# Batch 1's retention steps moved ahead inside batch 0's second product, on a one-core retention-and-mixer kernel

## The chip, the cores and the metric

The kernel runs on one core of a Trainium2 chip. The metric is device time in microseconds (us), the median of several executions. One further execution was taken with the hardware profiler; all rows quoted below are from it. The engines are named as in the profile: PE is TensorE's matrix multiply and PEld its weight load, DVE is VectorE, ACT is ScalarE, POOL is GpSimd, SP is SyncE (here only a queue that issues DMA transfers).

## The reference

```python
# q, k, v: (4, 8, 768, 64): batch, heads, sequence, head size
gamma = 1.0 - 2.0 ** (-5.0 - np.arange(H))
for t in range(S):                                   # retention, a recurrent state per head
    state = gamma * state + k[:, :, t] (outer) v[:, :, t]
    y[:, :, t] = 1/sqrt(D) * q[:, :, t] @ state
x = y.transpose(0, 2, 1, 3).reshape(B, S, H * D)     # (4, 768, 512)
h = x.transpose(0, 2, 1) @ U @ V                     # low-rank mixing along the sequence, rank 32
u = x + h.transpose(0, 2, 1)
out = u + relu(u @ w_ch1) @ w_ch2                    # 512 -> 2048 -> 512
```

## The kernel before

The sequence of 768 is cut into six chunks of 128 rows. For a chunk `c` of batch `b`, retention does the following steps.

- `ret_in`: GpSimd scales the loaded keys and queries by powers of gamma (`ret_k`, L257, writes `kd`; `ret_q`, L262, writes `qd`). For batch 1 and chunks 2, 3 and 4 it also queues on SP the loads of batch 2's chunks 0, 1 and 2 (`load_chunk`).
- `ret_T` (L424): eight PE transposes put `qd` and `kd` into one PSUM bank; `evict` copies them to the tile `qkT`, on ACT or DVE, whichever a small cost model (`Balance.pick`) expects to be done first.
- `ret_S` (L437): eight matmuls give the scores in two banks; DVE masks them into `a` (L446).
- `ret_v` (L268): ACT casts the values to `vb`.
- `ret_O`: matmuls give the chunk's outputs from the running state and from `a` and `vb`, and add to the state's sum; ACT evicts the outputs to `x` (L463), DVE evicts the state (L482).

After all six chunks of a batch come its mixing steps (`mix_P`, `mix_n`, `mix_u`), and then the two products of the mixer. The first product (`mlp1`) has 32 slots. The second has 42: three sets of row blocks (`i` = 0, 1, 2), each with seven products of half-size blocks in the order 4, 5, 1, 2, 3, 7, 6, each product split into two slots of four matmuls of 256 columns. A set's additions are shared out: ACT copies products 4, 5, 1 and 2 from PSUM (L642), GpSimd adds 5, 1 and 2 in four adds and one late add (L646), and DVE adds 3, 7 and 6 straight from PSUM (L646). Ahead of the second product DVE forms sums of the weights (`w2_sum`, L578) and of the activations (`g_sums`, L593).

Everything is issued in program order on every engine, and the program order comes from a table: `weave` runs through the slots, and ahead of each slot emits the actions that `put` has hung on it. So batch 1's retention is laid between the slots of batch 0's second product. In the table `at` gives the slot of each chunk's transposes, `lead` how many slots ahead `ret_in` is emitted, `S_at` and `O_at` the slots of scores and outputs, and `mix_at` the start of mixing; `n1` is 32, the first slot of the second product. `ret_v` goes three slots ahead of `O_at`. An action that is emitted later on GpSimd's queue runs later there, whether or not its inputs have long been there. POOL and SP have one queue each.

In what follows "slot 11" means slot `n1 + 11`, and T0, S0 and O0 are the transposes, scores and outputs of batch 1's chunk 0.

Of the kernel before, what the change touches and what calls it, by code (L numbers as in the profile page):

```python
# [47 lines left out]
def kernel(  # L48
# [52 lines left out]
    def set_banks(main, mix=None):  # L101

        for who, banks in (("main", main), ("mix", mix)):
            use[who] = banks and sorted(banks, key=lambda i: taken.get(i, 0))
            n_use[who] = 0
# [33 lines left out]
    def load_chunk(b, c, kinds="kqv"):  # L139
        t = staged.setdefault((b, c), {})  # L140
        for nm in kinds:
            load_one(t, b, c, {"k": k, "q": q, "v": v}[nm], nm + "_n")
# [8 lines left out]
    def load_w1(lo, w):  # L151
        nc.gpsimd.dma_start(
            out=w1b[:, :, ds(lo, w)],
            in_=moe_w_ch1[:, ds(lo, w)].rearrange("(c p) m -> p c m", p=P))

    def load_w2(s):
        nc.gpsimd.dma_start(
            out=w2b[:, ds(4 * s, 4)],
            in_=moe_w_ch2[ts(s, 512)].rearrange("(j p) c -> p j c", p=P))
# [9 lines left out]
    for what in ("q0", "kA", "q1", "k2", "k3", "vA", "q2", "k4", "v2", "k5", "v3", "v4", "v5"):  # L169
        src, i = {"q": q, "k": k, "v": v}[what[0]], what[1]  # L170
# [351 lines left out]
    def by_token(b, j):  # L522
        return b >= 2 or (b == 1 and j >= NCK // 2)
# [6 lines left out]
    def mix_r(b, j):  # L530
        h = mm_bank("mix")
        matmul(h, Vb[:, ts(j, P)], Ps[b], DM, start=True, stop=True)
        nc.vector.tensor_tensor(res_of(b, j), h, xs[b, j], op=ALU.add)  # L533
        bal.book("V", 0.69)
# [17 lines left out]
    def mlp1_two(b, ms, hf):  # L552
        if b not in gTs:
            gTs[b] = gtp.tile([P, NM, S], bf16, tag="gT", name=f"gT_{b}")
        g = [mm_bank()[:, :HS] for _ in ms]
        for cs in ((0, 1), (2, 3)):
            for m, o in zip(ms, g):
                for c in cs:
                    matmul(o, w1b[:, c, ts(m, P)], uTs[b][:, c, ts(hf, HS)], HS, start=(c == 0),
                           stop=(c == NCB - 1))  # L560
        for m, o in zip(ms, g):
            evict(gTs[b][:, m, ts(hf, HS)], o, HS, relu=True)
# [9 lines left out]
    def w2_sum(i, h):  # L572
        b11, b12, b21, b22 = (x[:, ts(h, HM // 2)] for x in w2_quads())
        z = w2s[:, :, ts(h, HM // 2)]
        o, x, y, op = ((z[:, 2], b21, b22, ALU.add), (b21, b21, b11, ALU.subtract),
                       (z[:, 0], b11, b22, ALU.add), (z[:, 1], b11, b12, ALU.add),
                       (b12, b12, b22, ALU.subtract))[i]
        nc.vector.tensor_tensor(o, x, y, op=op)  # L578
        bal.book("V", 0.65)
# [3 lines left out]
    def g_sums(b, n, which=range(5), w=2):  # L583
        if b not in gss:
            gss[b] = sump.tile([P, 3, HM, HS], bf16, tag="gs", name=f"gs_{b}")
        g, s = gTs[b], gss[b]
        mu, ml = ds(w * n, w), ds(HM + w * n, w)
        a11, a12, a21, a22 = (g[:, m, ts(t, HS)] for t in (0, 1) for m in (mu, ml))
        sums = ((s[:, 2, mu], a11, a12, ALU.add), (s[:, 0, mu], a11, a22, ALU.add),
                (s[:, 1, mu], a21, a22, ALU.add), (a12, a12, a22, ALU.subtract),  # L590
                (a21, a11, a21, ALU.subtract))
        for o, x, y, op in (sums[i] for i in which):
            nc.vector.tensor_tensor(o, x, y, op=op)  # L593
            bal.book("V", 0.55)
# [4 lines left out]
    def free_from(banks):  # L599
        free_banks[:] = sorted(banks, key=lambda i: taken.get(i, 0))  # L600
# [82 lines left out]
    def mlp1_slots(b):  # L683
        if b == 0:
            ms = [m + x for m in range(0, HM, 2) for x in (0, 1, HM, HM + 1)]
            return [lambda m=m, hf=hf: mlp1(b, m, hf) for m in ms for hf in (0, 1)]
        early = [m + x * HM for m in range(HM // 2) for x in (0, 1)]
        late = [m + HM // 2 for m in early]
        return [lambda m=m, hf=hf: mlp1(b, m, hf)
                for m, hf in [(m, hf) for hf in (0, 1) for m in early]  # L690
                + [(m, hf) for m in late for hf in (0, 1)]]
# [19 lines left out]
    def put(side, i, f):  # L711
        side.setdefault(int(i), []).append(f)

    def ret_side(b, at, lead, S_at, O_at, side):


        for c in range(NCK):
            put(side, max(0, at[c] - lead), lambda c=c: ret_in(b, c))
            put(side, O_at[c] - 3, lambda c=c: ret_v(b, c))
        for cs in S_at:  # L720
            put(side, S_at[cs], lambda cs=cs: ret_S(b, cs))
        for f, when in ((ret_T, at), (ret_O, O_at)):
            for c in range(NCK):
                put(side, when[c], lambda c=c, f=f: f(b, c))
        if by_dma(b) and b + 1 < B:
            for c, i in enumerate((31, 36, 41)):
                put(side, i, lambda c=c: load_chunk(b + 1, c))
        return side
# [67 lines left out]
    for b in range(B):  # L796
        nxt = b + 1 < B
        slots = mlp1_slots(b)
        n1 = len(slots)
        side = {}  # L800
        set_banks([0, 1, 2, SA, SB, OB])
        if b == 0:
            taken.update({i: n for n, i in enumerate((1, 2, 0, OB, SA, SB, TP))})
            set_banks([1, 2, 0, OB, SA, SB, TP])
            slots[:4] = [lambda: mlp1_two(0, (0, 1), 0), lambda: None,
                         lambda: mlp1_two(0, (0, 1), 1), lambda: None]
            for i, s in ((1, 512), (2, DH // 2 + 512)):
                put(side, i, lambda s=s: load_w1(s, 512))
            for n, s in enumerate((0, 2, 1, 3)):
                put(side, 4 + n, lambda s=s: load_w2(s))  # L810
            for c, nm in ((0, "kq"), (1, "kq"), (2, "kq"), (0, "v"), (3, "kq"), (1, "v"), (4, "kq"),
                          (2, "v"), (3, "v"), (5, "kq"), (4, "v"), (5, "v")):
                put(side, 14, lambda c=c, nm=nm: load_chunk(1, c, nm))
            for j, i in enumerate((4, 6, 8, 13, 14, 15)):
                put(side, i, lambda j=j: mix_r(0, j))
            for n, i in enumerate((9, 17, 25)):
                put(side, i, lambda n=n: g_sums(0, n))
            for i in range(5):
                put(side, 22, lambda i=i: w2_sum(i, 0))
            for i in (0, 1):  # L820
                put(side, n1 - 2, lambda i=i: w2_sum(i, 1))
            for f, *args in ((g_sums, 0, 3, (0, 1)), (w2_sum, 2, 1), (g_sums, 0, 3, (2,)),
                             (w2_sum, 3, 1), (w2_sum, 4, 1), (g_sums, 0, 3, (3, 4))):
                put(side, n1, lambda f=f, args=args: f(*args))
            at, lead, mix_at = [n1 + i for i in (11, 14, 18, 22, 26, 30)], 4, n1 + 36
            S_at = {(c,): n1 + i for c, i in enumerate((14, 17, 21, 25, 29, 33))}
            O_at = [n1 + i for i in (18, 21, 25, 29, 33, 36)]
        if b == 1:
            slots[:2] = [lambda: mlp1_two(1, (0, HM), 0), lambda: None]
            for j in range(NCK):  # L830
                if not by_token(1, j):
                    put(side, 6 + 3 * j, lambda j=j: mix_r(1, j))
        if b:
            for n, i in enumerate((13, 17, 25, n1)):
                put(side, i, lambda n=n: g_sums(b, n))
        if b and nxt:
            set_banks([0, 1, 2, TP])
            put(side, 22, lambda: set_banks([0, 1, 2]))
            at, lead, mix_at = [10 + 4 * c for c in range(NCK)], 5, n1 + 21
            S_at = {(0, 1): 27, (2,): 36, (3,): 40, (4,): 44, (5,): 48}  # L840
            O_at = [31, 34, 41, 45, 49, 53]
        banks = [[0, 1, 2], [0, 1, 2, TP], [0, 1, 2, TP], [0, 1, 2, TP, SA, SB, OB, ST]][b]
        put(side, n1, lambda: free_from(banks))
        if nxt:
            ret_side(b + 1, at, lead, S_at, O_at, side)
            put(side, mix_at, lambda: use.update(mix=[SA, SB, OB] + [TP] * (b == 0)))
            mix_side(b + 1, mix_at, side)
        if b in (1, 2):
            for c, i in ((3, 0), (4, 7), (5, 15)):
                put(side, i, lambda c=c: load_chunk(b + 1, c))  # L850
        weave(slots + mlp2_slots(b), side)
# [30 lines left out]
```

## Time and profile before

| | |
|---|---|
| median of 3 executions | 231.03 us (230.79 to 231.48) |
| profiled execution, its own time | 230.28 us |
| its span, first to last instruction | 228.5 us |
| PE busy | 215.0 us, 94% |
| DVE / ACT / POOL busy | 143.2 / 128.4 / 102.6 us |
| granted TensorE clock, mean over the span | 0.986 |

The time of an execution holds the span and 1.8 us around it. In the rows of a timeline the columns are the start in us from the span's start, the length in us, engine, line, operation, output and inputs with their shapes, and the count of instructions merged in the row; a bracket gives the idle time of that engine in front of the row and what ended it. PE's lengths are modelled and overlap: how long a piece of PE work takes is read from its start to the start of the next row. A row of the waits gives who waited for whom, the total, the number of times and the longest. A row of the windows gives a stretch of time, its length, busy time and count for PE, PEld, DVE, ACT and POOL, the granted clock (1.00 is full), the DMA share and GB/s.

### The profile page before, as it was taken

The page shows a single profiled execution, that of the slowest core. Times are in us where ns is not written, and L with a number is a line of the kernel's source. Part 1 is how long each engine was busy: PE and PEld are TensorE (multiplying, and loading weights), DVE is VectorE, ACT ScalarE, POOL GpSimd, SP SyncE. Part 2 cuts the span into 40 slices and gives each one's busy share as a digit, 9 for nine tenths or more (in the row PEclk, how much of TensorE's full clock was granted, in tenths as well). Part 3 has the DMA queues.
Part 4 walks back from the last instruction along what each step waited for, and adds up shares of the span by engine and source line. Part 5 has one row for each costly group of instructions (what it writes and reads, how often), then busy time and mean ns, then how long its engine had stood idle before and what let it go on. Part 6 is the DMA issues. An engine that isn't in the chain of part 4 may idle for free.

```text
span 228.5 us, 5097 instructions
## 1 busy us (share of the span) xinstructions
PE 215.0 (94%) x1997; PEld 151.2 (66%) x1999; DVE 143.2 (63%) x287; ACT 128.4 (56%) x267; POOL 102.6 (45%) x125
## 2 busy tenths in 40 slices
PE   7999999995798998999999999999999999999990
PEld 2566655664586874565788685657887865668890
DVE  8497668988278653298895633578983623555113
ACT  3377657762164647676646547776544757772220
POOL 6756910008959395332152359633606230006550
PEclk9999999999799999999999999999999999999997
DMA  6998999999999924999959988979560550000222
GB/s 173 244 261 172 168 174 207 200 219 225 205 260 227 232 84 127 193 161 173 107 123 221 261 168 154 227 132 171 101 132 3 161 160 4 1 0 3 93 92 93
DMA packets 100776, 34.90 MB, mean 153 GB/s; under 512 B 87152, under 2 KB 97808, under 8 KB 100752
## 3 DMA queue, kind: packets, MB, share of 16 engines
q1 hardware_dynamic: 94640, 30.29, 63.9%
q0 software_dynamic: 6112, 4.29, 12.9%
q8 instruction: 15, 0.25, 0.5%
q14 instruction: 9, 0.07, 0.1%
HBM read 27.46 MB, written 6.29 MB: 148 GB/s over the span
## 4 chain that ended last, share of the span: by engine, by line
PE 63%; POOL 11%; issue 10%; DMA 4%; DVE 4%; ACT 3%; SPq 3%; POOLq 0%; DVEq 0%; ACTq 0%
PE bk L116 61%; POOL s L646 4%; POOL res L646 4%; DMA k_n<-in_k_dram 2%; POOL qd L262 2%; DMA q_n<-in_q_dram 2%; SPq L288 2%; POOL kd L257 1%; SPq L136 1%; PE bk L424 1%; DVE a L352 1%; ACT st L299 1%; DVE res L646 1%; ACT x L538 1%; ACT kT L299 1%
## 5 line engine op out<-in xcount | busy, mean ns | idle before, releaser
L116 PE MATMUL bk<-uT,w1b 128*128 128x384 bf16 x512 | 86.4, 326 | 0.7 <-ACT uT L121 0.6
L121 ACT ACTIVATE gT<-bk 128x384 bf16<-128x384 f32 x123 | 60.1, 490 | 30.0 <-PE bk L116 29.9
L116 PEld LDWEIGHTS <-w1b 128*128 128x128 bf16 x512 | 49.8, 98 | 34.4 <-issue 1.6
L646 POOL TENSOR_TENSOR s<-s,s 128x256 f32<-128x256 f32 x24 | 18.2, 758 | 87.5 <-ACT s L642 65.1
L116 PEld LDWEIGHTS <-gT 128*128 128x128 bf16 x392 | 37.3, 99 | 8.4 <-issue 1.7
L593 DVE TENSOR_TENSOR gs<-gT 128x768 bf16<-128x768 bf16 x48 | 27.7, 614 | 20.8 <-ACT gT L121 20.3
L646 DVE TENSOR_TENSOR res<-bk,res 128x256 f32<-128x256 f32 x37 | 14.4, 420 | 28.1 <-PE bk L116 23.1
L116 PEld LDWEIGHTS <-gs 128*128 128x128 bf16 x288 | 27.3, 98 | 3.9
L257 POOL TENSOR_TENSOR kd<-k_n,Gk 128x512 bf16<-128x512 f32 x18 | 19.0, 1056 | 16.8 <-DMA k_n<-in_k_dram 11.1
L116 PE MATMUL bk<-w2b,gT 128*128 128x256 bf16 x192 | 26.4, 273 | 0.1
L116 PE MATMUL bk<-w2b,gs 128*128 128x256 bf16 x192 | 26.2, 273 | 0.0
L116 PE MATMUL bk<-w2s,gT 128*128 128x256 bf16 (+1 forms) x200 | 26.2, 277 | 0.0
L446 DVE TENSOR_TENSOR a<-bk,mask 128x512 bf16<-128x512 f32 x36 | 23.0, 684 | 4.8 <-PE bk L116 4.8
L642 ACT ACTIVATE s<-bk 128x256 f32<-128x256 f32 x36 | 13.5, 381 | 17.8 <-PE bk L116 17.3
L262 POOL TENSOR_TENSOR qd<-q_n,Gq 128x512 bf16<-128x512 f32 x18 | 19.8, 1098 | 5.7 <-DMA qkT<-qd 3.9
L533 DVE TENSOR_TENSOR res<-bk,x 128x512 f32<-128x512 f32 x24 | 15.8, 686 | 7.9 <-PE bk L116 7.6
L646 POOL TENSOR_TENSOR res<-res,s 128x256 f32<-128x256 f32 x24 | 17.9, 747 | 1.9
L593 DVE TENSOR_TENSOR gT<-gT 128x768 bf16<-128x768 bf16 x32 | 18.2, 609 | 0.0
L463 ACT ACTIVATE x<-bk 128x512 bf16<-128x512 f32 x18 | 10.7, 596 | 13.1 <-PE bk L116 10.4
L538 ACT ACTIVATE x<-res 128x512 bf16<-128x512 f32 x15 | 9.2, 628 | 6.3 <-DVE res L533 6.3
L116 PE MATMUL bk<-w2s,gs 128*128 128x256 bf16 x96 | 12.6, 273 | 0.0
L116 PEld LDWEIGHTS <-qkT 64*128 64x128 bf16 (+1 forms) x204 | 8.4, 95 | 4.7 <-issue 2.9
(98 smaller groups left out, 229.1 us busy)
## 6 DMA issues: line engine op xcount, KB each, us to landing
out_dram<-res SPq DMA_DIRECT2D x23, 256.0 KB, 2.3
k_n<-in_k_dram SPq DMA_DIRECT2D x22, 256.0 KB, 5.0
v_n<-in_v_dram SPq DMA_DIRECT2D x22, 256.0 KB, 4.7
q_n<-in_q_dram SPq DMA_DIRECT2D x18, 256.0 KB, 5.1
w2b<-in_moe_w_ch_dram POOLq DMA_DIRECT2D x4, 512.0 KB, 15.1
in<-in_q_dram SPq DMA_DIRECT2D x3, 512.0 KB, 6.4
w1b<-in_moe_w_ch_dram POOLq DMA_DIRECT2D x4, 256.0 KB, 5.5
w1b<-in_moe_w_ch_dram POOLq DMA_DIRECT2D x2, 512.0 KB, 9.0
```

The source lines that it names most:

```text
L116: nc.tensor.matmul(o, l, r, **kw)
L121: nc.scalar.activation(o, i, AF.Relu if relu else AF.Copy)
L257: eng.tensor_tensor(kd, k_n, Gk[:, c].unsqueeze(2).to_broadcast([P, H, D]), op=ALU.mult)
L262: eng.tensor_tensor(qd, rc[b, c]["q_n"], Gq[:, c].unsqueeze(2).to_broadcast([P, H, D]), op=ALU.mult)
L288: nc.sync.dma_start_transpose(out=qkT[:, i], in_=src.rearrange("p h d -> p (h d)"))
L446: nc.vector.tensor_tensor(r["a"][:, e], r["s"][e].rearrange("p (n t) -> p n t", n=NP), mask4, op=ALU.mult)
L463: nc.scalar.activation(x_of(b, c), o, AF.Copy)
L533: nc.vector.tensor_tensor(res_of(b, j), h, xs[b, j], op=ALU.add)
L538: nc.scalar.activation(xs[b, j], res[b, j], AF.Copy)
L593: nc.vector.tensor_tensor(o, x, y, op=op)
L642: nc.scalar.activation(t[nm], o, AF.Copy)
L646: eng.tensor_tensor(o, x, y, op=op)
```

## The change

Only the table for batch 1 inside batch 0's second product changes. The transposes move from slots 11, 14, 18, 22, 26, 30 to 8, 12, 16, 20, 25, 29; the lead grows from 4 to 5, so that `ret_in` moves from slots 7, 10, 14, 18, 22, 26 to 3, 7, 11, 15, 20, 24. The scores move from 14, 17, 21, 25, 29, 33 to 11, 15, 19, 23, 28, 32; the outputs from 18, 21, 25, 29, 33, 36 to 15, 19, 22, 27, 31, 35; mixing from 36 to 35. No instruction is added or taken away as computation.

```diff
-            at, lead, mix_at = [n1 + i for i in (11, 14, 18, 22, 26, 30)], 4, n1 + 36
-            S_at = {(c,): n1 + i for c, i in enumerate((14, 17, 21, 25, 29, 33))}
-            O_at = [n1 + i for i in (18, 21, 25, 29, 33, 36)]
+            at, lead, mix_at = [n1 + i for i in (8, 12, 16, 20, 25, 29)], 5, n1 + 35
+            S_at = {(c,): n1 + i for c, i in enumerate((11, 15, 19, 23, 28, 32))}
+            O_at = [n1 + i for i in (15, 19, 22, 27, 31, 35)]
```

GpSimd's queue from the first instruction after the weight loads, before. A name such as `kd_1_0` is the scaled keys of batch 1, chunk 0; `s4`, `s5`, `s1`, `c21` are copies of products of a set; `res_0_3` is a row block of batch 0's result.

```order
L646 TENSOR_TENSOR s5_952<-s4_941,s5_952 128x256
L646 TENSOR_TENSOR res_0_0_669<-res_0_0_669,s5_952 128x256
L646 TENSOR_TENSOR s1_965<-s1_965,s5_952 128x256
L646 TENSOR_TENSOR res_0_3_744<-res_0_3_744,s1_965 128x256
L257 TENSOR_TENSOR kd_1_0_973<-k_n_1_0_752,Gk_157 128x512
L262 TENSOR_TENSOR qd_1_0_975<-q_n_1_0_755,Gq_156 128x512
L646 TENSOR_TENSOR res_0_3_744<-res_0_3_744,c21_981 128x256
L257 TENSOR_TENSOR kd_1_1_994<-k_n_1_1_758,Gk_157 128x512
L262 TENSOR_TENSOR qd_1_1_996<-q_n_1_1_760,Gq_156 128x512
```

And the same place now:

```order
L257 TENSOR_TENSOR kd_1_0_948<-k_n_1_0_752,Gk_157 128x512
L262 TENSOR_TENSOR qd_1_0_950<-q_n_1_0_755,Gq_156 128x512
L646 TENSOR_TENSOR s5_956<-s4_941,s5_956 128x256
L646 TENSOR_TENSOR res_0_0_669<-res_0_0_669,s5_956 128x256
L646 TENSOR_TENSOR s1_969<-s1_969,s5_956 128x256
L646 TENSOR_TENSOR res_0_3_744<-res_0_3_744,s1_969 128x256
L257 TENSOR_TENSOR kd_1_1_977<-k_n_1_1_758,Gk_157 128x512
L262 TENSOR_TENSOR qd_1_1_979<-q_n_1_1_760,Gq_156 128x512
L646 TENSOR_TENSOR res_0_3_744<-res_0_3_744,c21_985 128x256
L257 TENSOR_TENSOR kd_1_2_1013<-k_n_1_2_762,Gk_157 128x512
L262 TENSOR_TENSOR qd_1_2_1015<-q_n_1_2_764,Gq_156 128x512
```

Chunk 0's pair of scalings now stands in front of the first set's four adds; chunk 1's pair takes the place that chunk 0's had, behind them, and the late add of `c21` comes after it. Further down, chunk 3's pair now stands in front of the second set's adds and chunk 4's behind four of them (before, chunk 3's stood between the second and the third add).

ACT's queue from the copies of the first set's products on, before:

```order
L642 ACTIVATE c21_981<-bk1_90_932 128x256
L121 ACTIVATE qkT_1_0_1011<-bk3_93_1002 128x1024
L121 ACTIVATE qkT_1_1_1061<-bk3_96_1052 128x1024
L268 ACTIVATE vb_1_0_1068<-v_n_1_0_766 128x512
L642 ACTIVATE s4_1074<-bk2_97_1063 128x256
L642 ACTIVATE s5_1098<-bk0_98_1076 128x256
```

And now:

```order
L642 ACTIVATE c21_985<-bk1_90_932 128x256
L121 ACTIVATE qkT_1_0_997<-bk3_93_988 128x1024
L268 ACTIVATE vb_1_0_1042<-v_n_1_0_766 128x512
L121 ACTIVATE qkT_1_1_1053<-bk3_96_1044 128x1024
L463 ACTIVATE x_1_0_1107<-bk6_100_1093 128x512
L642 ACTIVATE s4_1115<-bk2_97_1065 128x256
L268 ACTIVATE vb_1_1_1117<-v_n_1_1_773 128x512
L121 ACTIVATE qkT_1_2_1128<-bk3_102_1119 128x1024
L642 ACTIVATE s5_1139<-bk0_103_1130 128x256
```

The cost model now gives chunk 2's and chunk 5's `qkT` to ACT, where both were copies of DVE (L125); the two engines' other work keeps its engine.

On SP's queue three loads of batch 2 now stand in front of two stores of batch 0:

```order
+L136 DMA k_n_2_0_1017<-in_k_dram 128x8x64
+L136 DMA q_n_2_0_1019<-in_q_dram 128x8x64
+L136 DMA v_n_2_0_1021<-in_v_dram 128x8x64
 L674 DMA out_0_dram<-res_0_0_669 128x512
 L681 DMA out_0_dram<-res_0_3_744 128x512
-L136 DMA k_n_2_0_1033<-in_k_dram 128x8x64
-L136 DMA q_n_2_0_1035<-in_q_dram 128x8x64
-L136 DMA v_n_2_0_1037<-in_v_dram 128x8x64
```

The loads moved by two places; the rest of that queue keeps its order but for one store and one transposing transfer at the end of the stage, which change places.

## The prediction

> **What bounds the kernel now.** I read the page first, then the waits, then the timelines of PE and POOL around the one place where PE stands still for long, and last the granted clock by windows.
>
> ```profile
> PE 215.0 (94%) x1997; PEld 151.2 (66%) x1999; DVE 143.2 (63%) x287; ACT 128.4 (56%) x267; POOL 102.6 (45%) x125
> PE bk L424 <- POOL qd L262: 4.6, 3, 3.6
> ```
>
> PE is busy for 94% of the span, so only its stops and its clock can be won. The largest wait is that of the transposes for GpSimd's scaled queries: 4.6 us in three waits. PE's timeline has them all in the stage of the change:
>
> ```profile
> 53.15 1.24 PE L116 MATMUL bk<-w2b,gT 128*128 128x256 bf16 x8
> 54.23 0.60 PE L116 MATMUL bk<-w2s,gT 128*128 128x256 bf16 x4
> 58.38 0.61 PE L424 MATMUL bk<-ident,qd 128*128 128x128 bf16 x4 [3.55 <-POOL qd L262]
> 58.78 0.63 PE L424 MATMUL bk<-ident,kd 128*128 128x128 bf16 x4
> 59.21 2.74 PE L116 MATMUL bk<-w2s,gT 128*128 128x256 bf16 x12
> 61.89 0.40 PE L116 MATMUL bk<-qkT 64*128 64x128 bf16 x8
> 62.22 0.40 PE L424 MATMUL bk<-ident,qd 128*128 128x128 bf16 x4
> 62.68 1.04 PE L116 MATMUL bk<-w2b,gT 128*128 128x256 bf16 x8
> 63.55 0.60 PE L116 MATMUL bk<-w2b,gs 128*128 128x256 bf16 x4
> 69.18 0.40 PE L424 MATMUL bk<-ident,qd 128*128 128x128 bf16 x4 [0.39 <-POOL qd L262]
> 71.37 0.40 PE L116 MATMUL bk<-state,qkT 128*128 128x128 bf16 x4
> 72.06 0.60 PE L116 MATMUL bk<-w2s,gT 128*128 128x256 bf16 x4
> 73.36 0.40 PE L424 MATMUL bk<-ident,qd 128*128 128x128 bf16 x4 [0.70 <-POOL qd L262]
> 86.29 0.33 PE L116 MATMUL bk<-ident,x 128*128 128x128 bf16 x3 [0.18 <-DVE res L533]
> 87.93 4.28 PE L116 MATMUL bk<-uT,w1b 128*128 128x384 bf16 x24 [0.55 <-ACT uT L121]
> ```
>
> T0 waits 3.55 us, T3 0.39, T4 0.70; the stage's end, batch 1's mixing, costs 0.18 + 0.55. From start to start a half product (four matmuls) takes (63.55 − 62.68) / 2 = 0.44, a T 62.68 − 62.22 = 0.46, an S 62.22 − 61.89 = 0.33, an O 72.06 − 71.37 = 0.69. The 12 matmuls at 59.21 take 2.68 where three halves are 1.31. The clock tells why:
>
> ```profile
> 55.00:58.30 3.30, 0.00 (x0) 0.00 (x0) 1.51 (x3) 0.00 (x0) 3.22 (x5) 1.00 1.11 229
> 58.40:61.80 3.40, 3.40 (x20) 2.47 (x20) 0.42 (x1) 1.02 (x1) 3.40 (x4) 0.50 0.83 185
> 82.00:88.00 6.00, 5.11 (x45) 3.23 (x45) 3.94 (x8) 3.13 (x7) 6.00 (x8) 1.00 0.23 65
> 222.30:225.60 3.30, 1.01 (x18) 0.83 (x15) 2.14 (x7) 0.00 (x0) 0.20 (x1) 1.00 0.26 92
> 225.70:228.50 2.80, 0.00 (x0) 0.00 (x0) 0.00 (x0) 0.00 (x0) 0.00 (x0) 0.50 0.23 68
> ```
>
> Right behind the wait PE gets half its clock for 3.4 us, which costs another 3.4 × 0.5 = 1.7 us. What T0 waits for is on POOL:
>
> ```profile
> 52.08 1.12 POOL L646 TENSOR_TENSOR s<-s,s 128x256 f32<-128x256 f32 x1 [22.41 <-DVE gs L593]
> 53.28 1.05 POOL L646 TENSOR_TENSOR res<-res,s 128x256 f32<-128x256 f32 x1
> 54.30 1.03 POOL L646 TENSOR_TENSOR s<-s,s 128x256 f32<-128x256 f32 x1
> 55.41 0.92 POOL L646 TENSOR_TENSOR res<-res,s 128x256 f32<-128x256 f32 x1
> 56.29 1.04 POOL L257 TENSOR_TENSOR kd<-k_n,Gk 128x512 bf16<-128x512 f32 x1
> 57.29 1.04 POOL L262 TENSOR_TENSOR qd<-q_n,Gq 128x512 bf16<-128x512 f32 x1
> 58.29 0.72 POOL L646 TENSOR_TENSOR res<-res,c 128x256 f32<-128x256 f32 x1
> ```
>
> POOL is idle for 22.41 us, then does the first set's four adds, and only then the pair that T0 needs.
>
> **The change part by part.**
>
> Chunk 0's pair goes in front of the adds and can run when its inputs have landed:
>
> ```profile
> 38.34 0.37 SPq L136 DMA_DIRECT2D k_n<-in_k_dram  x1
> k_n<-in_k_dram SPq DMA_DIRECT2D x1, 256.0 KB, 9.7
> 38.80 0.53 SPq L136 DMA_DIRECT2D q_n<-in_q_dram  x1
> q_n<-in_q_dram SPq DMA_DIRECT2D x1, 256.0 KB, 10.3
> q_n<-in_q_dram SPq DMA_DIRECT2D x18, 256.0 KB, 5.1
> ```
>
> Keys land at 38.34 + 9.7 = 48.0, queries at 38.80 + 10.3 = 49.1, so the pair runs from 48.0 to about 50.1. The adds still begin at 52.08, and T0, now at 53.15, waits for nothing. The pair now lies beside DVE's sums:
>
> ```profile
> 48.59 0.69 DVE L578 TENSOR_TENSOR w2b<-w2b 128x1024 bf16<-128x1024 bf16 x1
> 52.65 1.10 DVE L578 TENSOR_TENSOR w2b<-w2b 128x1024 bf16<-128x1024 bf16 x1
> ```
>
> The same sum takes 0.69 us with POOL idle and 1.10 beside an add, and the add 1.12 instead of 0.72. The pair may so last from 2.0 to about 3.1 us (ending by 51.2, still ahead of 52.08) and make DVE 0 to 0.8 us late; PE's next wait covers that, so I take 0. Without that cover it would cost up to 0.8.
>
> **The wait goes to T1.** Chunk 1's pair inherits chunk 0's place behind the adds. It ends where chunk 0's ended, 57.29 + 1.04 = 58.33. From 53.15 PE has T0 0.46, product 3 0.87, half of 7 0.44, S0 0.33, the other half 0.44: it stands at T1 at 55.7 and waits 58.38 − 55.7 = 2.7 us. This takes 0.85 off the 3.55, no more. A late DVE would stretch the adds by up to 0.3. Behind T1 on PE stand product 6 and the second set; ACT waits with them for `qkT`.
>
> **The clock.** Is 2.7 us enough to lose it again? In this trace it changes at 58.4, 61.8 and 225.7; the last two lie 163.9 us = 48 × 3.41 apart, so it is decided at marks 3.41 us apart. At 225.7 it fell although PE had worked 1.01 of the 3.3 us ahead. In 82 to 88 PE had 15% idle and it stayed. On the same marks the gap of 55.7 to 58.4 fills 2.7 of the 3.4 us ahead of the mark at 58.4: 21% busy, nearer to the 31% that fell than to the 85% that stayed. So I take the full 1.7 again. The bounds are 0 and 1.7.
>
> **The later chunks.** Behind T1 (0.46) come product 6 (0.87), a half (0.44), S1 (0.33), O0 (about 0.5, being without a state part) and a half (0.44), 3.0 in all: T2 is reached at 61.4 or later; its pair is ready by 58.33 + 0.7 + 2.1 = 61.1. T3's 0.39 goes, since chunk 3's pair now precedes the second set's adds. T4's pair follows four of those. From the end of product 1 it needs two copies' time on ACT (about 1.0, at 0.38 to 0.60 each), two adds of 0.72 and the pair of 2.1, 4.5 in all; PE has T3, three products' worth of halves less one (5 × 0.44), O2 and S3 until then, 3.7, with small drains 3.9. I take a wait of 0.4 (0 to 0.7). Chunk 2's `qkT` goes from DVE to ACT:
>
> ```profile
> 65.72 0.68 DVE L125 COPY qkT<-bk 128x1024 bf16<-128x1024 bf16 x1
> 59.46 1.02 ACT L121 ACTIVATE qkT<-bk 128x1024 bf16<-128x1024 bf16 x1 [5.72 <-PE bk L424]
> ```
>
> It takes 1.02 instead of 0.68, behind two other ACT pieces of 0.4 and 0.6, for an S2 that comes 1.3 us after T2's end: 0 to 0.6, I take 0.15. Chunk 5's has 2.0 us until S5: nothing.
>
> **Product 3** took 54.23 − 53.15 = 1.08 for 0.87 of work, since a weight sum was late; T0 in front of it hides those 0.2. **The end:** two of three `mix_n` go one slot ahead, so DVE's last residual ends about 0.3 earlier, of which PE sees 0.1: 0.73 becomes 0.65. **SP:** batch 2's first loads go ahead of two stores that nothing waits for: 0.
>
> Sum. Lost now: 3.55 + 1.7 + 0.39 + 0.70 + 0.2 + 0.73 = 7.3. Lost then: 2.7 + 1.7 + 0.15 + 0.4 + 0.65 = 5.6. The gain is 1.7 us, by the bounds 0.8 to 2.4. Behind 87.93 PE waits for nothing up to its end, so the gain reaches the end: 230.28 − 1.7 = 228.6 for the profiled execution. That one lies 0.75 below the median; I carry the difference over, 231.03 − 1.7 = 229.3.
>
> **The rivals.**
>
> *The clock stays full.* With the gap shorter than one stretch between marks, or cut by a mark, the 1.7 falls away and T2 to T4 wait as above: a gain of 3.3, so 227.7. Against it stands the fall at 225.7 after 31% of work; for it, that the marks may lie elsewhere in other executions. The Trainium skill, "TensorE: Matmul & The Clock Gate", section "What's actually happening", says that the clock halves after at least one idle window of about 3.4 us and that the windows run freely; by that rule a gap of 2.7 us could never cost the clock. The trace agrees on the window's length, 3.4 us, and speaks against the need for a whole idle one at 225.7.
>
> *The gain is eaten.* If T4's wait grows to 0.7, ACT's longer queue delays S2 by 0.6 and DVE's lateness adds 0.3 at T1, there are 0.8 left, and a little more of the same in the drains makes it no change: 230.6.
>
> *Slower, by a late load.* Chunk 0's pair now bars the adds. If the queries land so late that the pair ends after 52.08, the adds, chunk 1's pair and T1 are late by as much. The gain of 1.7 is used up when the pair ends at 53.8, the queries landing at 52.7, 13.9 us after issue instead of 10.3; two us later still it is 233. For it: this load took twice the median of its 18 fellows, 5.1, so it already lies in a crowd. Against it: 3 us of margin.
>
> **How the numbers follow.** Forecast 0.62, full clock 0.18, eaten 0.13, slower 0.07. A difference below 0.3%, 0.7 us, can't be told from none. Of the forecast's 0.62 some 0.58 lie beyond that; with 0.18, and 0.03 of the eaten case, faster has 0.79. Same has 0.04 + 0.10 = 0.14, slower 0.07. The forecast's own range is 228.6 to 230.2. Mine reaches down to the full clock's 227.7 and up to 230.6.
>
> **What would show it.** Right: POOL's first pair at 48 to 51; T0 at 53.2 without a wait; T1 with a wait of 2.4 to 3.0 ended by `qd` at 58.3 to 58.7; behind it about 3.4 us at a clock of 0.50; no wait at T3; mlp1 of batch 1 starting 1.7 us earlier than 87.93. Wrong: a clock of 1.00 behind T1 (then 3.3), a first add after 52.3 (late load), or PE waits for `qkT` in front of S2 or S5.

## The result, and the profile after

The changed kernel takes 228.04 us (median of 4 executions, 227.4 to 228.12) against 231.16 us before (230.79 to 231.48): a ratio of 0.986, 95% interval 0.9836 to 0.9883. It is 3.1 us faster; the forecast was a gain of 1.7 and a time of 229.3.

The span, from the page of the kernel after, and a row of its waits:

```profile
span 226.1 us, 5100 instructions
PE bk L424 <- POOL qd L262: 1.7, 2, 1.3
```

POOL's timeline of the same execution at the place of the change (start, duration, operation, and in brackets the idle time before it with what ended it):

```profile
48.08 1.23 POOL L257 TENSOR_TENSOR kd<-k_n,Gk 128x512 bf16<-128x512 f32 x1 [18.55 <-DMA k_n<-in_k_dram]
49.29 1.48 POOL L262 TENSOR_TENSOR qd<-q_n,Gq 128x512 bf16<-128x512 f32 x1
52.13 0.73 POOL L646 TENSOR_TENSOR s<-s,s 128x256 f32<-128x256 f32 x1 [1.36 <-ACT s L642]
```

And PE's, in the same columns:

```profile
52.30 0.60 PE L116 MATMUL bk<-w2s,gs 128*128 128x256 bf16 x4 [0.23 <-DVE w2s L578]
53.61 0.39 PE L424 MATMUL bk<-ident,qd 128*128 128x128 bf16 x4
55.58 0.60 PE L116 MATMUL bk<-w2b,gT 128*128 128x256 bf16 x4 [0.93 <-DVE w2b L578]
58.80 0.40 PE L424 MATMUL bk<-ident,qd 128*128 128x128 bf16 x4 [1.31 <-POOL qd L262]
64.03 0.40 PE L116 MATMUL bk<-qkT 64*128 64x128 bf16 x8 [0.21 <-ACT qkT L121]
69.80 0.40 PE L424 MATMUL bk<-ident,qd 128*128 128x128 bf16 x4 [0.40 <-POOL qd L262]
84.44 4.28 PE L116 MATMUL bk<-uT,w1b 128*128 128x384 bf16 x24 [0.55 <-ACT uT L121]
```

Chunk 0's pair runs at 48.1, T0 at 53.6 waits for nothing, and T1 now waits for `qd` until 58.80. PE's standstill ahead of T1 comes in two pieces: inside product 3, for a late weight sum of DVE, and in front of T1. S2 waits 0.21, T3 not at all, T4 0.40. Batch 1's first product starts at 84.44 instead of 87.93, a gain of 3.49 in the stage.

The clock is what the forecast missed. Two stretches of the windows after:

```profile
53.62:57.04 3.42, 2.49 (x32) 1.89 (x30) 3.38 (x4) 1.93 (x3) 3.34 (x4) 1.00 1.14 228
57.04:60.45 3.41, 2.10 (x23) 1.69 (x22) 3.11 (x7) 0.99 (x1) 3.41 (x5) 1.00 0.77 155
```

The granted clock is 1.00 in both; there is no stretch at 0.50 behind T1. And 1.1 us of the gain is lost again far behind the change, in batch 1's second product:

```profile
129.15 1.04 PE L116 MATMUL bk<-w2b,gs 128*128 128x256 bf16 x8
131.33 1.03 PE L116 MATMUL bk<-w2b,gT 128*128 128x256 bf16 x8 [1.14 <-ACT s L642]
```

DVE's timeline of the same execution there shows what it waits for, a store:

```profile
129.02 1.32 DVE L533 TENSOR_TENSOR res<-bk,x 128x512 f32<-128x512 f32 x2 [1.32 <-DMA out_dram<-res]
```

The span so falls by 228.5 − 226.1 = 2.4 us between the two profiled executions; the medians, over executions that differ among themselves, lie 3.1 apart.

### The profile page after: what moved, and what is told of

Read it like the earlier page. It is cut to its first block, busy times and chain, and to the rows that moved or that the text cites. A ratio compares the mean times of both kernels' runs of the same rounds, so it can differ in the third digit from the quotient of the medians.

```text
span 226.1 us, 5100 instructions
## 1 busy us (share of the span) xinstructions
PE 212.7 (94%) x1997; PEld 150.2 (66%) x1999; DVE 145.4 (64%) x285; ACT 130.5 (58%) x269; POOL 103.5 (46%) x125
## 4 chain that ended last, share of the span: by engine, by line
PE 62%; issue 9%; POOL 8%; DMA 7%; SPq 7%; ACT 3%; DVE 2%; POOLq 0%; DVEq 0%; ACTq 0%
PE bk L116 61%; DMA v_n<-in_v_dram 3%; POOL res L646 3%; POOL s L646 3%; SPq L136 2%; SPq L166 2%; DMA k_n<-in_k_dram 2%; DMA q_n<-in_q_dram 2%; SPq L288 2%; POOL kd L257 2%; POOL qd L262 1%; DVE res L646 1%; PE bk L424 1%; ACT st L299 1%; ACT s L642 1%
## 5 line engine op out<-in xcount | busy, mean ns | idle before, releaser
L116 PEld LDWEIGHTS <-gT 128*128 128x128 bf16 x392 | 36.5, 98 | 10.2 <-issue 3.7
L593 DVE TENSOR_TENSOR gs<-gT 128x768 bf16<-128x768 bf16 x48 | 28.7, 636 | 19.6 <-ACT gT L121 19.2
L257 POOL TENSOR_TENSOR kd<-k_n,Gk 128x512 bf16<-128x512 f32 x18 | 19.8, 1103 | 34.8 <-DMA k_n<-in_k_dram 29.4
L116 PE MATMUL bk<-w2b,gT 128*128 128x256 bf16 x192 | 26.9, 273 | 2.1 <-ACT s L642 1.1
L116 PE MATMUL bk<-w2s,gT 128*128 128x256 bf16 (+1 forms) x200 | 25.3, 268 | 0.0
L593 DVE TENSOR_TENSOR gT<-gT 128x768 bf16<-128x768 bf16 x32 | 19.4, 646 | 0.0
L482 DVE TENSOR_TENSOR state<-bk,bmask 128x512 bf16<-128x512 f32 x15 | 10.3, 688 | 4.1 <-PE bk L116 4.1
```

The source lines that it names most:

```text
L116: nc.tensor.matmul(o, l, r, **kw)
L257: eng.tensor_tensor(kd, k_n, Gk[:, c].unsqueeze(2).to_broadcast([P, H, D]), op=ALU.mult)
L482: nc.vector.tensor_tensor(sb, ps.rearrange("p (n t) -> p n t", n=NP), bmask4, op=ALU.mult)
```

## The experiments

All ratios are to the kernel before, run beside it on the same chip.

**The pair alone** (everything else in its old slot):

```diff
-            put(side, max(0, at[c] - lead), lambda c=c: ret_in(b, c))
+            put(side, n1 + 3 if (b, c) == (1, 0) else max(0, at[c] - lead), lambda c=c: ret_in(b, c))
```

> The kernel before with one thing changed: chunk 0's pair of scalings is emitted at slot 3, in front of the first set's adds; every other step keeps its old slot. Theory A (the gain is T0's wait plus the 1.7 us of half clock behind it, and both fall with the pair alone): PE waits about 1.9 us for DVE's late sum inside product 3, T0 waits for nothing, T1 waits about 1.1; the clock stays at 1.00; batch 1's first product starts near 85.0 instead of 87.9 and the time is 228.5 (228.0 to 229.3). Rival B (the earlier slots of all the other steps carry the gain, the pair alone does little): at most half of the 3.1 us, 229.6 or more.

Measured: 228.39 us, ratio 0.9878 (0.9806 to 0.995). PE's timeline:

```profile
56.23 0.60 PE L116 MATMUL bk<-w2b,gT 128*128 128x256 bf16 x4 [1.37 <-DVE w2b L578]
57.10 0.39 PE L424 MATMUL bk<-ident,qd 128*128 128x128 bf16 x4
60.14 0.40 PE L424 MATMUL bk<-ident,qd 128*128 128x128 bf16 x4 [0.78 <-POOL qd L262]
71.26 0.40 PE L424 MATMUL bk<-ident,qd 128*128 128x128 bf16 x4 [0.69 <-POOL qd L262]
85.83 4.28 PE L116 MATMUL bk<-uT,w1b 128*128 128x384 bf16 x24 [0.55 <-ACT uT L121]
```

In the stage theory A holds: T0 (57.10) waits for nothing, and the standstill is again in two pieces, 1.37 and 0.78, with a clock of 1.00. T4's 0.69 of the kernel before is still there. The stage ends 2.1 of the 3.5 us earlier (85.83), in an execution whose second product had also begun 0.35 late behind a weight load. Yet this profiled execution took 230.24 us, as long as the 230.28 of the kernel before: PE gave the 2.1 back in two later waits, 0.95 at 132.52 (again for ACT, with DVE in front of it waiting 1.1 for the store) and 1.15 for a transposing transfer:

```profile
136.45 17.71 PE L116 MATMUL bk<-uT,w1b 128*128 128x384 bf16 x108 [1.15 <-DMA uT<-x]
```

The other three executions took 227.14 to 229.22. Rival B's 229.6 lies inside the upper half of the interval, so the time alone does not exclude it; what speaks against it is the end of the stage in the trace.

**The rest without the pair** (the changed table, the pair at slot 7, behind the adds):

```diff
-            put(side, max(0, at[c] - lead), lambda c=c: ret_in(b, c))
+            put(side, n1 + 7 if (b, c) == (1, 0) else max(0, at[c] - lead), lambda c=c: ret_in(b, c))
```

> The changed kernel, but chunk 0's pair goes back behind the first set's four adds; all transposes, scores, outputs and the mixing keep their earlier slots. Theory A: T0, now at 53.6, waits for the pair until 58.4, some 4.8 us, and the clock falls behind it as before (1.7); T1 waits little. Lost in the stage 5.0 + 1.7 + 0.2 + 0.4 + 0.6 = 7.9 against 7.3 before, so the time is 231.2 to 232.4, not faster than before. Rival B: faster than before by 1 us or more, 230.1 or less.

Measured: 231.15 us, ratio 1.0006 (0.9967 to 1.0044), no gain at all. T0 in PE's timeline:

```profile
58.33 0.61 PE L424 MATMUL bk<-ident,qd 128*128 128x128 bf16 x4 [5.05 <-POOL qd L262]
```

And two of its windows, with the granted clock as the last but two number:

```profile
52.12:55.53 3.41, 1.16 (x11) 0.79 (x9) 3.38 (x4) 0.77 (x2) 3.25 (x4) 1.00 1.30 222
55.60:62.30 6.70, 3.97 (x28) 2.84 (x28) 0.85 (x3) 1.54 (x2) 6.70 (x8) 0.50 1.34 220
```

T0 comes sooner and waits longer for a pair that is done when it was done before, and the clock is at 0.50 for 6.7 us, of which PE stands still for some 2.7. The earlier slots are worth something only once the pair is in front.

**The clock's price by itself** (the kernel before, with idle matmuls in PE's wait; the new helper `fill`, not shown here, issues them and leaves the cost model's count for PE as it was):

```diff
+            put(side, n1 + 11, lambda: fill(14))    # 14 idle matmuls of 512 columns, ahead of T0
```

> The kernel before with 14 idle matmuls of 512 columns (about 3 us at full clock, their result is thrown away) in front of T0, in the time in which PE waits for the pair anyway; nothing else is moved. Theory A (the half clock behind T0 is a cost of its own of 1.7 us, and the timed executions of the kernel before had it too): the clock stays at 1.00 behind T0, T0 still starts near 58.4, and the time falls to 229.4. Rival C (the half clock is the profiled execution's own, or costs nothing): the time stays at 231.1.

Measured: 229.69 us, ratio 0.9937 (0.9912 to 0.9962), so 0.9 to 2.0 us faster by nothing but work that is thrown away. PE's timeline, with the idle matmuls and T0:

```profile
55.24 2.97 PE L116 MATMUL bk<-idle 128*128 128x512 bf16 x13
58.74 0.40 PE L429 MATMUL bk<-ident,qd 128*128 128x128 bf16 x4 [0.53 <-POOL qd L267]
```

The window behind T0:

```profile
58.80:62.20 3.40, 2.97 (x39) 2.46 (x40) 1.92 (x4) 1.14 (x2) 3.40 (x4) 1.00 0.67 147
```

T0 is not earlier; the clock behind it is 1.00. Each execution also has a mean clock, and (1 − clock) × 2 × span is its time at half clock; the end behind the last matmul gave up to 3.1 us of it in the traces. All 10 executions of this kernel have 2.7 us or less, 17 of the 19 of the kernel before beside it have 3.7 or more. So nearly every execution of the kernel before paid, and rival C falls. The two profiled executions lie only 0.4 apart (229.84 and 230.28): against the 1.7 saved stand T0's start 0.36 later, a wait of 0.43 at T1 and waits of 0.31 and 0.16 behind the stage.

**One gap instead of two** (two of DVE's weight sums exchanged; sum 3 then reads a block that sum 4 has changed, so the numbers of batch 0's product 6 are others, while the work is the same):

```diff
-                             (w2_sum, 3, 1), (w2_sum, 4, 1), (g_sums, 0, 3, (3, 4))):
+                             (w2_sum, 4, 1), (w2_sum, 3, 1), (g_sums, 0, 3, (3, 4))):
```

> The changed kernel with two of DVE's weight sums exchanged, so that the one that product 3 waits for (0.93 us) comes about 1.1 us earlier. Theory A: T1 still starts when chunk 1's pair is done, about 58.8, so the wait in product 3 only moves into T1's, which grows from 1.3 to about 2.2 us in one piece; time unchanged, 228.0, if the clock bears a gap of 2.2 us, and 229.7 with a stretch of half clock if it does not. Rival D (the two waits are independent costs): 0.9 us faster, 227.1.

> The kernel with the exchanged weight sums again (sum 3 then reads a block that sum 4 has already changed, so its numbers are not the reference's; the work and its length are the same), with more executions, for the clock alone. Theory A (the clock is decided on marks 3.41 us apart whose place differs from execution to execution, and falls where most of one stretch is idle): with one gap of 2.5 us some executions, about half, show a mean clock under 0.992 and are 1.4 to 1.9 us longer than the others. Rival (only a wholly idle stretch of 3.4 us lowers it): none does; the executions differ no more than the changed kernel's.

Measured: 228.02 us, ratio 0.9860 (0.9802 to 0.9919), and 228.44 us, 0.9879 (0.9832 to 0.9925). The waits moved as theory A had it:

```profile
58.71 0.40 PE L424 MATMUL bk<-ident,qd 128*128 128x128 bf16 x4 [2.49 <-POOL qd L262]
```

This row is of the first measurement. T1 starts where it did; product 3's 0.93 is now in front of it, and rival D falls. The executions split into two groups. The five with 1.4 us or less at half clock took 227.1 to 227.9 us; the five with 3.6 to 6.3 took 228.7 to 230.0. Half of them lost the clock, and these are 0.8 to 2.9 us longer (expected: 1.4 to 1.9). The profiled execution of the first measurement kept its clock in spite of the 2.49 in one piece; there a mark fell into the gap, at 57.14. The profiled one of the second lost it at 59.54, behind a stretch in which PE waited 0.41 and 1.82 us and was still busy for 1.18:

```profile
56.13:59.54 3.41, 1.18 (x14) 0.86 (x14) 3.41 (x6) 0.10 (x1) 3.41 (x4) 1.00 0.99 199
```

That stretch was not wholly idle, so the second rival falls too.

**The changed kernel again**, as the control in two sets of runs (the first with the two edits below, alone and together; the second with the loads, both edits and the exchanged sums):

> The changed kernel itself once more, on the chip of the three others: about 3.1 us faster than the kernel before (ratio 0.984 to 0.988), the clock at 1.00 up to the last matmul in every execution, and some 0.5 to 1.2 us of PE's wait at 130.

> The changed kernel itself, beside the three others: near 228.2, ratio to the kernel before 0.984 to 0.989; a mean clock of 0.993 or more in nearly all executions, since PE's standstill lies in two pieces of 1.1 and 1.5 us.

Measured: 228.37 us (ratio 0.9876, 0.9825 to 0.9927) and 228.22 us (0.9868, 0.983 to 0.9905). The expectation on the clock was a miss: of the 14 executions of this kernel in all, three have 3.6 to 5.5 us at half clock. The profiled one of the second set is one of these. Its PE timeline:

```profile
54.70 0.60 PE L116 MATMUL bk<-w2b,gT 128*128 128x256 bf16 x4 [0.38 <-DVE w2b L578]
58.60 0.40 PE L424 MATMUL bk<-ident,qd 128*128 128x128 bf16 x4 [2.00 <-POOL qd L262]
```

And its windows on either side of the mark at 59.38:

```profile
55.97:59.38 3.41, 1.41 (x19) 1.07 (x16) 2.86 (x6) 0.12 (x1) 3.41 (x5) 1.00 0.86 183
59.40:62.78 3.38, 3.38 (x31) 2.31 (x29) 1.12 (x3) 1.04 (x2) 3.38 (x4) 0.50 1.07 228
```

Here PE waited only 0.38 for DVE's sum, T1's wait was 2.00 in one piece, and the half clock of the forecast followed, 3.4 us of it.

**Loads behind the stores** (batch 3's chunk 2, aimed at the wait at 130):

```diff
-            for c, i in enumerate((31, 36, 41)):
+            for c, i in enumerate((31, 36, 46 if b == 2 else 41)):
```

> The changed kernel; in batch 1's second product the three loads of batch 3's chunk 2 are queued on SP at slot 46 instead of 41, behind the two stores of the first set. Theory (the 1.14 us that PE loses at 130 comes from the store of batch 1's row block 3, which stands on SP behind nine loads, and DVE's residual needs that block's buffer): the store goes out about 3 us earlier, PE's wait at 130 falls to under 0.2, the time falls by 1.0 to about 227.0. Rival (PE would wait there anyway, for ACT's queue or for the next transfers): less than 0.4 gained.

> The changed kernel with the loads of batch 3's chunk 2 behind the two stores, with more executions: if the wait at 130 is there in most executions of the changed kernel and gone here, 0.6 to 1.0 us faster than the changed kernel beside it. Rival: the stores' lateness differs from execution to execution, and the medians differ by less than 0.4.

SP's timeline of the changed kernel at the store for which DVE waits at 129:

```profile
125.94 0.37 SPq L681 DMA_DIRECT2D out_dram<-res  x1
```

SP's timeline with the loads moved, and then DVE's:

```profile
123.24 0.37 SPq L681 DMA_DIRECT2D out_dram<-res  x1
```

```profile
127.26 2.48 DVE L533 TENSOR_TENSOR res<-bk,x 128x512 f32<-128x512 f32 x4
```

The store is issued 2.7 us earlier, DVE no longer waits, and PE has no wait at 130 in the traces of both measurements; from batch 1's first product to the span's end this kernel takes 225.8 − 85.27 = 140.5 us where the changed one took 226.1 − 84.44 = 141.7. The times say less: 228.37 us in the first measurement (ratio 0.9864, 0.9802 to 0.9925), equal to the control, where 227.0 was expected, and 227.26 in the second (ratio 0.9831, 0.979 to 0.987) against 228.22. The cause of the wait is shown; the size of the gain, 0 to 1.0, is not settled.

**Chunk 1's pair in front too**, alone and with the loads moved:

```diff
-            put(side, max(0, at[c] - lead), lambda c=c: ret_in(b, c))
+            put(side, n1 + 3 if b == 1 and c < 2 else max(0, at[c] - lead), lambda c=c: ret_in(b, c))
```

> The changed kernel; chunk 1's pair too is emitted at slot 3, behind chunk 0's and in front of the first set's adds. Theory (what is left in the stage is T1's wait for a pair behind the adds, plus DVE's sums late beside the pairs): the pairs run from 48 to about 53.4, the adds end 1.3 us later, T1 waits for nothing and starts near 57.5 instead of 58.8, PE's wait inside product 3 grows from 0.9 to 1.0 to 1.5, T2 waits up to 0.3; the stage ends about 1.0 us earlier. At most 1.0 faster than the changed kernel, less what is given back at 130. Rival (the pairs only push the adds and DVE's sums back by as much as they win): same as the changed kernel, 228.0.

> Both edits together: chunk 1's pair in front of the adds, and batch 3's chunk 2 loads behind the two stores. Theory: the two waits are in different places, so both gains add, some 2 us under the changed kernel, near 226.1. Rival: with PE earlier, another transfer (the transposes of batch 2's x) ends last at 130 to 136 and holds it near 227.

> Chunk 1's pair in front of the adds too, and the loads behind the stores, with more executions. The pairs move the waits from T1 to DVE's sums and win nothing by themselves (2.6 us of waits in the stage instead of 2.5); with the loads' gain the time is 0.4 to 1.0 under the changed kernel.

Measured: alone 228.50 us (0.9876, 0.9833 to 0.992), next to 228.37 of the control: nothing won.

```profile
53.57 0.60 PE L116 MATMUL bk<-w2s,gs 128*128 128x256 bf16 x4 [1.73 <-DVE w2s L578]
56.83 0.60 PE L116 MATMUL bk<-w2b,gT 128*128 128x256 bf16 x4 [0.91 <-DVE w2b L578]
```

T1's wait is gone, and PE waits 1.73 us for DVE's sums in product 1 and 0.91 in product 3 instead, 2.6 in all where the changed kernel has 2.5: the rival was right. With the loads moved it takes 227.65 us (0.9844, 0.981 to 0.9878) and 227.10 (0.9832, 0.9792 to 0.9872), the lowest median of each set, 0.7 and 1.1 under the control. The 226.1 of two gains added was missed, since the second pair by itself won nothing. The interval overlaps the control's, so that it beats the changed kernel is likely and not shown.

## Why the prediction was right or wrong

**Right: the bound and what the pair does.** The pair ran at 48.1, the adds began at 52.13, T0 waited for nothing, the wait went to T1, which started at 58.80 (forecast 58.3 to 58.7). Its wait was 1.31 instead of 2.4 to 3.0, since PE had stood still before it for DVE. The two halves of the change, taken apart, show that the pair carries it: alone 0.9878, the rest without it 1.0006.

**Right: the terms of the later chunks.** S2 0.21 (taken 0.15), T3 nothing, T4 0.40 (taken 0.4), the end 0.55 (taken 0.65).

**The number was in part luck.** The time lies in the stated range because that range reached down to the rival's 227.7; the forecast's own 228.6 to 230.2 missed it. For the stage the rival of the full clock, which got 0.18, was the nearer: its gain of 3.3 stands against 3.49.

**Wrong: "So I take the full 1.7 again".** This is the step that failed, and with it the choice between the forecast and that rival. It took the gap as one piece ahead of a mark at 58.4, the place of the mark in the trace of before. The marks differ between executions: they lay at 57.04 and 60.45 in the profiled execution after, at 59.38 in the last control. But it is not their place that kept the clock after the change. Wherever a stretch of 3.41 us is laid over the rows of that execution between 46 and 66 us, PE is busy for at least 1.91 us of it, 56%, and the highest share behind which the clock fell in any trace is 43%. The least busy stretch of the changed kernel, then that of the first measurement of the exchanged sums:

```profile
54.75:58.16 3.41, 1.91 (x20) 1.21 (x19) 3.41 (x5) 1.04 (x2) 3.33 (x4) 1.00 1.15 223
```

```profile
55.32:58.73 3.41, 0.92 (x14) 0.52 (x14) 3.03 (x6) 0.30 (x1) 3.33 (x5) 1.00 1.13 207
```

In the second kernel, whose gap is in one piece, PE's share goes down to 27%, so there it depends on the marks whether the clock falls. In the last control, which lost it, PE waited only 0.38 for DVE and then 2.00 in one piece; the least share there is 41%. The counts of executions that lost the clock, 3 of 14 and 5 of 10, point the same way and would be too few by themselves.

**Half wrong: "PE's next wait covers that, so I take 0".** The bound on DVE's lateness, 0.8, was too small: the sum for which product 3 waits started at 54.43 instead of 52.65, 1.8 late. The pair made DVE 0.7 late by 51.57, as bounded; this pushed the next sums beside GpSimd's adds, where they were longer too. In these rows of DVE after the change the first sum takes 1.21 instead of 0.69:

```profile
53.19 1.21 DVE L578 TENSOR_TENSOR w2s<-w2b 128x1024 bf16<-128x1024 bf16 x1
54.43 1.09 DVE L578 TENSOR_TENSOR w2b<-w2b 128x1024 bf16<-128x1024 bf16 x1
```

As a length the lateness was covered: PE waited 0.23 + 0.93 + 1.31, 2.5 in all, and the forecast's gap was 2.7. But it cut that gap in two, with 1.9 us of PE's work between (55.58 to 57.49), and so saved the 1.7. The lateness itself comes from the pair. DVE's timeline of the changed kernel, then of the kernel with the pair behind the adds:

```profile
48.45 1.42 DVE L578 TENSOR_TENSOR w2b<-w2b 128x1024 bf16<-128x1024 bf16 x1
```

```profile
48.42 0.69 DVE L578 TENSOR_TENSOR w2b<-w2b 128x1024 bf16<-128x1024 bf16 x1
```

Only the first of the two sums has the pair on POOL beside it. The Trainium skill, "GPSIMD Engine Reference", section "Specifications", says that GpSimd shares its SBUF interfaces with VectorE and contends with VectorE instructions that have two SBUF inputs; this sum has two, and the trace agrees, 1.42 us against 0.69.

**Wrong: "Behind 87.93 PE waits for nothing up to its end, so the gain reaches the end".** The reading of the trace before was right, and the inference was not. The stage won 3.49 us; PE, sooner by that, met a store that was sooner by only 128.40 − 125.94 = 2.5, behind nine loads on SP, and waited 1.14. In the trace before, DVE already waited for that store by 0.24 (SP's timeline, then DVE's):

```profile
128.40 0.37 SPq L681 DMA_DIRECT2D out_dram<-res  x1
```

```profile
131.45 1.31 DVE L533 TENSOR_TENSOR res<-bk,x 128x512 f32<-128x512 f32 x2 [0.24 <-DMA out_dram<-res]
```

That row was the warning: work off PE that ends just in time is no slack for a shift of 3 us. The errors on the clock and on the store have opposite signs; with the clock kept and the loss at 130 the forecast's own terms give 1.7 + 1.7 − 1.1 = 2.3, against 2.2 between the two profiled executions' own times (230.28 and 228.12).

**Wrong: "I carry the difference over".** The profiled execution lay 0.75 under the median before and 0.08 above it after. The forecast for the profiled execution, 228.6, was 0.5 off the 228.12 that came; the rest of the 1.3 by which the forecast of the median, 229.3, missed 228.04 comes from the difference carried over and from the two medians of before, 231.03 and 231.16. Why the medians moved further is not split here: half-clock time in the executions of before goes up to 9.7 us, so some of them lost more than the profiled one.

Two smaller points. By its own terms the eaten case leaves 1.7 − 0.3 − 0.45 − 0.3, about 0.65, where 0.8 is written. And a wait for `qkT` in front of S2, named as a sign of being wrong, did come, at 0.21, about as large as the 0.15 in the sum.

## What to carry to other kernels

A scaling that has its inputs long before it is issued belongs in front of adds that wait for PE, on an in-order queue, before anything that consumes it is moved. Look at how PE's idle time is cut up as well as how much there is: here 2.00 us in one piece cost 3.4 us at half clock behind it, 1.7 us more, and 0.93 and 1.31 with 1.9 us of work between them cost nothing more. Ahead of carrying a gain to the end, look for the waits of other engines that are just short of PE's path, such as a store that frees a buffer.

## What the runs showed of the hardware

The clock is decided on PE's busy share of stretches of 3.41 us, not on a wholly idle one. PE's busy time is the third number of a row of the windows, and its lengths are modelled. Two stretches just ahead of a mark, of the kernel with both pairs in front and the loads moved, in two executions:

```profile
50.93:54.34 3.41, 1.48 (x14) 0.98 (x12) 3.41 (x4) 0.49 (x2) 3.41 (x3) 1.00 1.17 229
```

```profile
50.73:54.14 3.41, 1.69 (x17) 1.36 (x14) 3.41 (x4) 0.64 (x2) 3.40 (x3) 1.00 1.18 233
```

Behind the first the clock fell at 54.34, behind the second it stayed. It fell behind 1.16 us (the rest without the pair) and 1.41 (the last control) and stayed at 2.10 (the changed kernel). The lowest share behind which it stayed in any trace is 48%, in the second of the two executions:

```profile
217.98:221.40 3.42, 1.63 (x23) 1.39 (x21) 2.14 (x7) 0.00 (x0) 0.74 (x2) 1.00 0.11 38
```

So all that was seen in 14 profiled executions puts the limit between 43% and 48% busy. The Trainium skill, "TensorE: Matmul & The Clock Gate", section "What's actually happening", asks for at least one idle window of 3.4 us; taken as a window without any work, the runs contradict that. They agree with it that the windows are 3.4 us long and run freely: the marks lie at other places in each profiled execution. That fits the exchanged sums, which lost the clock in five executions and kept it in five.
